# Giving the third x tile's transposes their own PSUM tiles and copies, at the start of a fused MLP forward and backward kernel

## The chip, the cores and the metric

The kernel runs on one NeuronCore of a Trainium2 chip. The metric is device time in microseconds (us), low is good. Each kernel was run several times; the median and the lowest and highest run are given. Where a ratio of two kernels is given, it is the mean time of one kernel's runs over the mean of the other's runs of the same rounds, with a 95% interval, so it is not quite the ratio of the medians quoted beside it. A profile is one execution recorded by the hardware profiler; its times count from the start of that execution's span.

## The reference

```python
B, S, D, F = 1, 2048, 640, 1536          # x, w1, w2, grad_out: bf16
def fwd(x, w1, w2):
    h = silu(einsum("bsd,df->bsf", x, w1))
    return einsum("bsf,fd->bsd", h, w2)
def reference(x, w1, w2, grad_out):
    out, vjp = jax.vjp(fwd, x, w1, w2)
    return (out, *vjp(grad_out))          # out, grad x, grad w1, grad w2
```

## The kernel before

The sequence is worked in four chunks of 512 rows. The first product, h = x w1, needs x transposed. For chunks 1 to 3 a DMA transposes it. For chunk 0 three x tiles of 128 rows are loaded plainly and transposed on TensorE (PE) against an identity; only the last 128 rows of the chunk come by DMA transpose (issued at 3.37 us in the trace of before, landing 4.9 us later, when the first matmul had long begun at 4.05). The first stage, `h_first`, then runs 40 matmuls of 384 columns, row block by row block of w1 (`dt_`), over eight output blocks (`ft`) at a time. The matmul that this document calls the ninth is the first one of the second w1 row block (`dt_ = 1`, `ft = 0`).

```python
P, NQ, SC, DT, NA, FC, FA = 128, 3, 512, 5, 8, 512, 1024
HC = NQ * P                                   # 384
# 18 warm-up matmuls on a tile of ones, from 0.51 to 2.61 us in the trace of before      ... cut
early += [load_x(nc.sync, 0), load_x(nc.scalar, 1), load_x(nc.sync, 2)]
early += [load_w1(0, slice(0, FC), nc.scalar), load_w1(0, slice(FC, FA))]
early += [load_w1(k, slice(0, FA)) for k in range(1, 3)]
for k in range(3, DT):
    load_w1(k, slice(0, FA))
nc.sync.dma_start_transpose(out=xT_next[:, :, HC:SC], in_=x2[HC:SC, :])
# ... cut: w2, grad_out and the transposed weights are loaded after these

def pe_x(xT):
    slices = ((0, 1), (1, 3), (3, DT))
    tps = [ps_h.tile([P, hi - lo, NQ, P], dt_in, name="tp", tag="hp") for lo, hi in slices]
    for q in range(NQ):
        for tp, (lo, hi) in zip(tps, slices):
            for dt_ in range(lo, hi):
                nc.tensor.transpose(tp[:, dt_ - lo, q, :], x_nat[:, q, dt_ * P:(dt_ + 1) * P], ident[:])
    for k, (tp, (lo, hi)) in enumerate(zip(tps, slices)):
        copy_tp = nc.scalar.copy if k % 2 else nc.vector.tensor_copy
        copy_tp(out=xT[:, lo:hi, 0:HC], in_=tp[:].rearrange("p k q s -> p k (q s)"))

def h_first(xT, aT, ghT):
    pe_x(xT)
    hs = [ps_h.tile([P, SC], FP32, name="hp") for _ in range(NA)]
    def mm(ft, dt_, cols, start, stop):
        nc.tensor.matmul(hs[ft][:, cols], lhsT=w1_nat[:, dt_, ft * P:(ft + 1) * P],
                         rhs=xT[:, dt_, cols], start=start, stop=stop)
    for dt_ in range(DT):
        for ft in range(NA):
            mm(ft, dt_, slice(0, HC), dt_ == 0, False)
    # ... cut: the last 128 columns, silu, the other four output blocks
```

## Time and profile before

| | before |
|---|---|
| time, first 3 runs | 320.03 us median (319.85 to 320.49) |
| span of the profiled execution | 317.7 us |
| PE busy | 313.2 us, 99% |

The first part of the page of the kernel before (busy us, share of the span and instructions of each engine) and its part on the chain of work that ended last:

```profile
PE 313.2 (99%) x1501; PEld 146.8 (46%) x1529; DVE 102.9 (32%) x182; ACT 77.2 (24%) x139; POOL 0.7 (0%) x6
...
PE 99%; issue 1%; DVE 0%; DVEq 0%
PE hp L299 32%; PE hp L283 16%; PE hp L388 16%; PE hp L439 15%; PE hp L220 13%; PE hp L251 3%; PE hp L419 1%; PE wp L162 1%; PE tp L211 0%; DVE xT L216 0%; DVE g L430 0%; DVE warm L158 0%; DVEq L430 0%; DVEq L467 0%
```

PE is busy for 99% of the span and the chain is PE from end to end. Time can be won only by giving PE less work, or by starting its useful work sooner. The change tries the second, so the first 6 us matter. The next fence is from the timeline of the kernel before (its first line is the heading: start in us, duration in us, engine, line, operation, output<-input, count, and in brackets the idle time before with what ended it). `tp` is the PSUM tile of the transposes, `w_nat` stands for w1 here (the profile leaves digits out of names), PEld is the weight load of the matmul that follows.

```profile
start us, us, engine line op out<-in xcount [idle before <-releaser]
...
2.43 1.39 PE L211 MATMUL tp<-ident,x_nat 128*128 128x128 bf16 x15
...
3.64 0.82 DVE L216 COPY xT<-tp 128x384 bf16<-128x384 bf16 x2 [3.19 <-PE tp L211]
3.73 0.10 PEld L251 LDWEIGHTS <-w_nat 128*128 128x128 bf16 x1
3.75 0.80 ACT L216 COPY xT<-tp 128x768 bf16<-128x768 bf16 x1 [1.06 <-PE tp L211]
4.05 9.15 PE L251 MATMUL hp<-xT,w_nat 128*128 128x384 bf16 x80 [0.23 <-DVE xT L216]
4.05 0.42 PEld L251 LDWEIGHTS <-w_nat 128*128 128x128 bf16 x3 [0.22 <-issue]
...
4.86 0.44 PEld L251 LDWEIGHTS <-w_nat 128*128 128x128 bf16 x4 [0.39 <-DMA w_nat<-in_w_dram]
...
5.59 7.44 PEld L251 LDWEIGHTS <-w_nat 128*128 128x128 bf16 x72 [0.29 <-DMA w_nat<-in_w_dram]
```

How to read it: the 15 transposes start at 2.43; the two DVE copies begin at 3.64 and the ACT copy at 3.75; the first 384-column matmul starts at 4.05, when the first DVE copy is done. After four weight loads (the one at 3.73 and three at 4.05) PE waits for a DMA until 4.86 (columns 512 to 1023 of the first w1 row block), and after four more it waits again until 5.59 (second row block). The 72 loads from there on show no wait. (In some fences below a count is cut at the end of the window that was asked for, as x43, or a record is missing from the trace, as in x79.)

Three numbers below this resolution come from the single records of the trace: the third x tile's DMA completed at 3.33; the first DVE copy (128x384) took 0.358 us and the second (128x768) 0.549; the two weight DMAs completed at 4.82 and 5.55.

### The profile page before, as it was taken

The page shows a single profiled execution, that of the slowest core. Times are in us where ns is not written, and L with a number is a line of the kernel's source. Part 1 is how long each engine was busy: PE and PEld are TensorE (multiplying, and loading weights), DVE is VectorE, ACT ScalarE, POOL GpSimd, SP SyncE. Part 2 cuts the span into 40 slices and gives each one's busy share as a digit, 9 for nine tenths or more (in the row PEclk, how much of TensorE's full clock was granted, in tenths as well). Part 3 has the DMA queues.
Part 4 walks back from the last instruction along what each step waited for, and adds up shares of the span by engine and source line. Part 5 has one row for each costly group of instructions (what it writes and reads, how often), then busy time and mean ns, then how long its engine had stood idle before and what let it go on. Part 6 is the DMA issues. An engine that isn't in the chain of part 4 may idle for free.

```text
span 317.7 us, 3605 instructions
## 1 busy us (share of the span) xinstructions
PE 313.2 (99%) x1501; PEld 146.8 (46%) x1529; DVE 102.9 (32%) x182; ACT 77.2 (24%) x139; POOL 0.7 (0%) x6
## 2 busy tenths in 40 slices
PE   9999999999999999999999999999999999999997
PEld 6644444444444444444444444444444444444444
DVE  1396631577310177700157741000000100001001
ACT  2592000654101354311064420111100001001110
POOL 0000000000000000000000000000000000000000
DMA  8989999999989885482644089919999999996011
GB/s 266 329 167 207 229 267 245 337 255 279 292 220 339 203 241 133 148 283 85 165 119 131 0 274 264 206 31 295 244 254 254 253 218 343 242 274 207 33 35 50
DMA packets 147264, 66.85 MB, mean 210 GB/s; under 512 B 113328, under 2 KB 146736, under 8 KB 147248
## 3 DMA queue, kind: packets, MB, share of 16 engines
q1 hardware_dynamic: 146960, 66.33, 82.0%
q10 hardware_dynamic: 288, 0.30, 0.3%
q8 instruction: 12, 0.20, 0.3%
q14 instruction: 4, 0.03, 0.0%
HBM read 9.18 MB, written 28.97 MB: 120 GB/s over the span
## 4 chain that ended last, share of the span: by engine, by line
PE 99%; issue 1%; DVE 0%; DVEq 0%
PE hp L299 32%; PE hp L283 16%; PE hp L388 16%; PE hp L439 15%; PE hp L220 13%; PE hp L251 3%; PE hp L419 1%; PE wp L162 1%; PE tp L211 0%; DVE xT L216 0%; DVE g L430 0%; DVE warm L158 0%; DVEq L430 0%; DVEq L467 0%
## 5 line engine op out<-in xcount | busy, mean ns | idle before, releaser
L283 PE MATMUL hp<-goT,w2T 128*128 128x512 bf16 x238 | 56.8, 380 | 0.1
L299 PE MATMUL hp<-aT,w_nat 128*128 128x512 bf16 x235 | 52.2, 379 | 0.3
L299 PE MATMUL hp<-ghT,w1T 128*128 128x512 bf16 x236 | 52.2, 379 | 0.2
L388 PE MATMUL hp<-a_blk,go_nat 128*128 128x512 bf16 x235 | 51.7, 379 | 0.3
L439 PE MATMUL hp<-gh_blk,x_nat 128*128 128x512 bf16 x220 | 48.3, 379 | 0.2
L220 PE MATMUL hp<-xT,w_nat 128*128 128x512 bf16 x192 | 47.8, 379 | 0.4
L307 ACT ACTIVATE oT<-hp 128x512 bf16<-128x512 f32 x24 | 14.4, 598 | 104.3 <-PE hp L299 104.3
L229 ACT ACTIVATE aT<-hp 128x512 bf16<-128x512 f32 x48 | 28.5, 614 | 37.2 <-PE hp L220 30.4
L283 PEld LDWEIGHTS <-w2T 128*128 128x128 bf16 x240 | 23.5, 98 | 28.3
L299 PEld LDWEIGHTS <-w_nat 128*128 128x128 bf16 x240 | 23.5, 98 | 28.3
L388 PEld LDWEIGHTS <-go_nat 128*128 128x128 bf16 x240 | 23.5, 98 | 28.3
L299 PEld LDWEIGHTS <-w1T 128*128 128x128 bf16 x240 | 23.4, 98 | 28.4
L290 DVE SCALAR_TENSOR_TENSOR ghT<-ghT,hp 128x512 bf16<-128x512 bf16 x48 | 32.5, 682 | 7.0 <-PE hp L283 7.0
L439 PEld LDWEIGHTS <-x_nat 128*128 128x128 bf16 x224 | 21.9, 98 | 26.5
L309 DVE CAST oT<-hp 128x512 bf16<-128x512 f32 x16 | 11.0, 690 | 70.6 <-PE hp L299 70.6
L236 DVE SCALAR_TENSOR_TENSOR ghT<-aT,v 128x512 bf16<-128x512 bf16 x48 | 32.6, 686 | 0.3
L220 PEld LDWEIGHTS <-w_nat 128*128 128x128 bf16 x200 | 19.5, 98 | 23.4
L235 DVE TENSOR_SCALAR v<-t 128x512 bf16<-128x512 f32 x48 | 20.1, 425 | 28.1 <-ACT t L233 28.1
L233 ACT ACTIVATE t<-hp 128x512 f32<-128x512 f32 x44 | 26.5, 620 | 0.0
L450 DVE CAST g<-hp 128x512 bf16<-128x512 f32 x7 | 4.8, 691 | 47.0 <-PE hp L439 28.2
L398 DVE CAST g2T<-hp 128x512 bf16<-128x512 f32 x7 | 4.8, 692 | 46.1 <-PE hp L388 46.1
L396 ACT ACTIVATE g2T<-hp 128x512 bf16<-128x512 f32 x8 | 4.8, 597 | 47.0 <-PE hp L388 47.0
(24 smaller groups left out, 42.0 us busy)
## 6 DMA issues: line engine op xcount, KB each, us to landing
aT_scr<-aT SPq DMA_DIRECT2D x4, 1536.0 KB, 6.2
ghT_scr<-ghT SPq DMA_DIRECT2D x4, 1536.0 KB, 8.0
out_dram<-o_sb SPq DMA_DIRECT2D x8, 640.0 KB, 3.7
oT_scr<-oT SPq DMA_DIRECT2D x4, 640.0 KB, 3.9
go_nat<-in_grad_out_dram SPq DMA_DIRECT2D x4, 640.0 KB, 7.7
gxT_scr<-oT SPq DMA_DIRECT2D x4, 640.0 KB, 5.2
w_nat<-in_w_dram SPq DMA_DIRECT2D x1, 1920.0 KB, 11.8
x_nat<-in_x_dram SPq DMA_DIRECT2D x3, 640.0 KB, 7.4
```

The source lines that it names most:

```text
L220: nc.tensor.matmul(hp[:], lhsT=w1_nat[:, dt_, ft * P:(ft + 1) * P], rhs=xT[:, dt_, :], start=(dt_ == 0), stop=(dt_ == DT - 1),)
L229: nc.scalar.activation(aT[:, ft, :], hp[:], ACT.Silu)
L233: nc.scalar.activation(t[:], hp[:], ACT.Tanh, scale=0.5)
L235: nc.vector.tensor_scalar(out=v[:], in0=t[:], scalar1=-0.5, scalar2=0.5, op0=ALU.mult, op1=ALU.add)
L236: nc.vector.scalar_tensor_tensor(out=ghT[:, ft, :], in0=aT[:, ft, :], scalar=1.0, in1=v[:], op0=ALU.subtract, op1=ALU.mult)
L283: nc.tensor.matmul(gp[:], lhsT=w2T[:, dt_, ft * P:(ft + 1) * P], rhs=goT[:, dt_, :], start=(dt_ == 0), stop=(dt_ == DT - 1),)
L290: nc.vector.scalar_tensor_tensor(out=ghT[:, ft, :], in0=ghT[:, ft, :], scalar=1.0, in1=gp[:], op0=ALU.add, op1=ALU.mult)
L299: nc.tensor.matmul(op_[:], lhsT=w_all[:, ft, dt_ * P:(dt_ + 1) * P], rhs=rhs_all[:, ft, :], start=(ft == 0), stop=(ft == FT - 1),)
L307: nc.scalar.activation(oT[:, dt_, :], op_[:], ACT.Copy)
L309: nc.vector.tensor_copy(out=oT[:, dt_, :], in_=op_[:])
L388: nc.tensor.matmul(gp[:], lhsT=go_nat[:, st, dt_ * P:(dt_ + 1) * P], rhs=a_blk[:, st, :], start=(st == 0), stop=(st == ST - 1),)
L439: nc.tensor.matmul(gp[:], lhsT=x_nat[:, st, dt_ * P:(dt_ + 1) * P], rhs=gh_blk[:, st, :], start=(st == 0), stop=(st == ST - 1),)
```

## The change

The third x tile arrives last. In the kernel before, one PSUM tile (the prediction says bank) holds all three tiles' transposes of the first row block, and one copy of 384 columns follows the last of them. The change copies the first two tiles' part ahead, while the third is still being transposed, so that after the last needed transpose a copy of only 128 columns stands before the first matmul. Four PSUM tiles are used for transposes in place of three.

```diff
-            slices = ((0, 1), (1, 3), (3, DT))
-            tps = [ps_h.tile([P, hi - lo, NQ, P], dt_in, name="tp", tag="hp") for lo, hi in slices]
-            for q in range(NQ):
+            slices = ((0, 1), (1, DT))
+            for qs in ((0, 1), (2,)):
+                tps = [ps_h.tile([P, hi - lo, len(qs), P], dt_in, name="tp", tag="hp") for lo, hi in slices]
+                for k, q in enumerate(qs):
+                    for tp, (lo, hi) in zip(tps, slices):
+                        for dt_ in range(lo, hi):
+                            nc.tensor.transpose(tp[:, dt_ - lo, k, :], ...)
                 for tp, (lo, hi) in zip(tps, slices):
-                    for dt_ in range(lo, hi):
-                        nc.tensor.transpose(tp[:, dt_ - lo, q, :], ...)
-            for k, (tp, (lo, hi)) in enumerate(zip(tps, slices)):
-                copy_tp = nc.scalar.copy if k % 2 else nc.vector.tensor_copy
-                copy_tp(out=xT[:, lo:hi, 0:HC], in_=...)
+                    copy_tp = nc.scalar.copy if lo and len(qs) > 1 else nc.vector.tensor_copy
+                    copy_tp(out=xT[:, lo:hi, qs[0] * P:(qs[-1] + 1) * P], in_=...)
```

(The elided arguments are as in the kernel before.) The instructions on PE keep their order.

More of the change, by code (lines that the diff above doesn't have):

```diff
@@ L205, in pe_x @@
         def pe_x(xT):
-            slices = ((0, 1), (1, 3), (3, DT))
-            tps = [ps_h.tile([P, hi - lo, NQ, P], dt_in, name="tp", tag="hp") for lo, hi in slices]
-            for q in range(NQ):
-                for tp, (lo, hi) in zip(tps, slices):
-                    for dt_ in range(lo, hi):
-                        nc.tensor.transpose(
-                            tp[:, dt_ - lo, q, :], x_nat[:, q, dt_ * P:(dt_ + 1) * P], ident[:]
-                        )
-            for k, (tp, (lo, hi)) in enumerate(zip(tps, slices)):
-                copy_tp = nc.scalar.copy if k % 2 else nc.vector.tensor_copy
-                copy_tp(out=xT[:, lo:hi, 0:HC], in_=tp[:].rearrange("p k q s -> p k (q s)"))
+            slices = ((0, 1), (1, DT))
[4 more added lines that the diff above has]
+                        for dt_ in range(lo, hi):
+                            nc.tensor.transpose(
+                                tp[:, dt_ - lo, k, :], x_nat[:, q, dt_ * P:(dt_ + 1) * P], ident[:]
+                            )
+                for tp, (lo, hi) in zip(tps, slices):
+                    copy_tp = nc.scalar.copy if lo and len(qs) > 1 else nc.vector.tensor_copy
+                    copy_tp(
+                        out=xT[:, lo:hi, qs[0] * P:(qs[-1] + 1) * P], in_=tp[:].rearrange("p k q s -> p k (q s)")
+                    )
         def h_mm(hp, ft, xT):
```

## The prediction

> **What bounds the kernel now.** The matmul engine: the profile's first table gives PE 313.2 of 317.7 us (99%), and the chain of waits is 99% PE. Only the start has anything to win. The timeline and its single records show (us from the span's start):
>
> - the third x tile lands at 3.33; its first transpose starts at 3.37; the transpose that the first copy needs ends at 3.60;
> - the first DVE copy, 128x384, runs 3.64 to 4.00 (0.358 us); the second, 128x768 in 0.549 us, ends at 4.46; the ACT copy, 128x768 in 0.798 us, ends at 4.55;
> - the first real matmul starts at 4.05, after that first copy; then one of 384 columns starts every 0.162 us;
> - the fifth needs columns 512 to 1023 of the first w1 row block. PE could take it at 4.70, but the DMA lands at 4.82 and the weight load starts at 4.86;
> - the ninth needs the second w1 row block. PE could take it at about 5.52; that DMA lands at 5.55, the load starts at 5.59.
> - After 5.59 no wait of PE in this stage is listed.
>
> **What the change does.** Transposes and matmuls stay the same, in the same order. The 384-column first copy becomes 256 + 128 columns on DVE; the two 128x768 copies become 128x1024 on ACT (first two x tiles) and 128x512 on DVE (third). Transposes use four PSUM banks, not three.
>
> Costs, estimated from the two DVE copies (about 0.17 us + 0.50 ns a column): 256 columns 0.29 us, done by 3.6, hidden under the third tile's transposes; 128 columns 0.23 us, 3.64 to 3.87; 512 columns 0.42 us, ending about 4.3. ACT, from 0.798 us for 768 columns and about 0.60 us for 512: 1.0 us for 1024, but starting 0.2 us sooner, so ending at about 4.55 as now. The first matmul then starts at about 3.92: 0.13 us sooner, not the 0.24 us of two thirds of the copy, because of DVE's fixed part.
>
> **How much is on the critical path.** Almost none. Four matmuls run 0.13 us earlier, then PE meets the same weights at 4.86 and 5.59; the wait before the fifth grows from 0.16 to about 0.29 us. The copies for the second row block are ready at 4.55, 1 us before its weights.
>
> On SP's queue one order changes, later: the first oT store goes ahead of the third chunk's xT load. Both come far ahead of use (that chunk starts near 108 us); I expect nothing.
>
> **Time.** 320.0 us before, 320.0 predicted; the gain is at most 0.13 us (0.04%), under the spread of the runs before (319.85 to 320.49). Range 319.6 to 320.4.
>
> **What would show it.** First 384-column matmul at about 3.9; the idle time before the fifth longer by as much; the ninth still at about 5.6, directly after its DMA; the span unchanged within 0.3 us.
>
> **What would make it wrong.** If in other executions the weights land over 0.2 us earlier against x, PE and not the DMA sets the ninth matmul, and the 0.13 us is saved. Also the clock: [...] Here transposes go from 0.106 to 0.055 us spacing at about 3.2; a later change would slow the first matmuls and take the DMA waits off the path. Either is worth tenths of a us.

## The result, and the profile after

| | before | after |
|---|---|---|
| median of 5 runs | 320.29 us (319.85 to 320.63) | 319.93 us (319.6 to 320.29) |
| ratio | | 0.9992, 95% interval 0.9978 to 1.0006 |
| span of the profiled execution | 317.7 us | 318.5 us |

The time is the same within the noise. Yet the profiled execution of the changed kernel was 0.8 us *longer* than that of the kernel before. The same parts of its page, and the same stretch of its timeline:

```profile
PE 315.5 (99%) x1529; PEld 147.5 (46%) x1529; DVE 103.0 (32%) x183; ACT 77.4 (24%) x139; POOL 0.7 (0%) x6
...
PE 98%; DMA 1%; DVE 0%; issue 0%; DVEq 0%; SPq 0%
PE hp L302 33%; PE hp L286 16%; PE hp L391 16%; PE hp L442 15%; PE hp L223 14%; PE hp L254 3%; PE hp L422 1%; DMA x_nat<-in_x_dram 1%; PE tp L212 1%; DVE g L433 0%; DVEq L433 0%; SPq L470 0%
```

(The first fence is the page, the second the timeline of the changed kernel.)

```profile
2.85 1.78 PE L212 MATMUL tp<-ident,x_nat 128*128 128x128 bf16 x15 [0.24 <-DMA x_nat<-in_x_dram]
...
3.72 0.29 DVE L217 COPY xT<-tp 128x256 bf16<-128x256 bf16 x1 [3.26 <-PE tp L212]
...
4.25 0.23 DVE L217 COPY xT<-tp 128x128 bf16<-128x128 bf16 x1 [0.24 <-PE tp L212]
...
4.53 9.50 PE L254 MATMUL hp<-xT,w_nat 128*128 128x384 bf16 x80
...
4.80 0.15 PEld L254 LDWEIGHTS <-w_nat 128*128 128x128 bf16 x1 [0.17 <-issue]
...
5.12 0.15 PEld L254 LDWEIGHTS <-w_nat 128*128 128x128 bf16 x1 [0.17 <-issue]
...
6.42 7.44 PEld L254 LDWEIGHTS <-w_nat 128*128 128x128 bf16 x72 [0.25 <-DMA w_nat<-in_w_dram]
```

(PE's busy time is not comparable between the two pages: the trace of before holds 1501 of the matmuls, that of after 1529.)

The change did what it was meant to do. DVE now copies 256 columns at 3.72, under the transposes, and the copy that the first matmul waits for takes 0.23 us (single record: 0.225, against 0.358). The first matmul starts 0.28 us after the start of that copy (4.25 to 4.53); before it was 0.41 us (3.64 to 4.05).

But nearly everything around it differs. The transposes start 0.42 us later because the first x tile landed later (at 2.81 in place of 2.39), and they take 1.78 us in place of 1.39. The weight loads from 4.80 on come 0.32 us apart, twice the 0.162 us of the kernel before. PE is at half clock: transposes start 0.107 us apart in place of 0.056, matmuls of 384 columns 0.320 in place of 0.162. ("Half clock" and "full clock" are names for these two spacings here. That the clock is behind them is a reading of the traces: the clock records of this trace begin at 5.71, with a granted share of 1.0, where the spacing falls to 0.162; there is none before, and the page counts that time as full clock. The trace of before has no clock record.) The single records show the change of speed: in this trace the half-clock spacing holds up to the matmul that starts at 5.12; in the trace of before, up to the transpose at 3.05. The fifth matmul's weights (DMA complete at 4.33) were not waited for at all. The ninth was: PE would have been free for it at about 6.39 (the eighth started at 6.23, plus 0.162), but its weights landed at 6.37 and its load started at 6.42. That is nearly a tie, 0.03 us: with the old copy, 0.133 us longer, PE would have come to the ninth matmul after its weights, so part of the saving (an estimate: at most 6.39 + 0.133 - 6.42 = 0.10 us) reached even this execution.

So two traces already show two things that set the ninth matmul's start and that the change does not touch: when PE leaves half clock, and when the weights land. The experiments ask which of them holds, how often, and whether the 0.13 us is there when neither does.

### The profile page after: what moved, and what is told of

Same layout as the page of the kernel before. It is cut to its first block, busy times and chain, and to the rows that moved or that the text cites. A ratio compares the mean times of both kernels' runs of the same rounds, so it can differ in the third digit from the quotient of the medians.

```text
span 318.5 us, 3634 instructions
## 1 busy us (share of the span) xinstructions
PE 315.5 (99%) x1529; PEld 147.5 (46%) x1529; DVE 103.0 (32%) x183; ACT 77.4 (24%) x139; POOL 0.7 (0%) x6
## 4 chain that ended last, share of the span: by engine, by line
PE 98%; DMA 1%; DVE 0%; issue 0%; DVEq 0%; SPq 0%
PE hp L302 33%; PE hp L286 16%; PE hp L391 16%; PE hp L442 15%; PE hp L223 14%; PE hp L254 3%; PE hp L422 1%; DMA x_nat<-in_x_dram 1%; PE tp L212 1%; DVE g L433 0%; DVEq L433 0%; SPq L470 0%
```

## The experiments

Three theories: A, the prediction's: the ninth matmul starts when the second w1 block lands, so a shorter copy only lengthens a wait. B: the first copy sets the start of the stage, and its saving reaches the end of every execution. C: the state at the start (clock, landings) is what moves the times from run to run.

The table collects all traces. "Half clock until" is the start of the last matmul or transpose that was followed at full half-clock spacing (0.105 us or more for 128 columns, 0.319 for 384); in the two traces marked "again" PE had been at full clock before and had fallen back (the last of the 110 warm-up matmuls ended by 9.00 and 8.83 us, under 0.08 us for each, less than the half-clock spacing of 0.107). All columns are us from the span's start, from the single records.

| trace | third x tile landed | half clock until | first matmul | second w1 block landed | ninth matmul | span |
|---|---|---|---|---|---|---|
| before | 3.33 | 3.05 | 4.05 | 5.55 | 5.60 | 317.7 |
| before_again | 3.51 | 5.74 | 4.51 | 4.90 | 6.67 | 318.7 |
| after | 3.63 | 5.12 | 4.53 | 6.37 | 6.42 | 318.5 |
| after_again | 3.58 | 4.04 | 4.35 | 5.38 | 5.67 | 317.7 |
| w_late | 3.47 | 3.81 | 4.25 | 7.92 | 7.96 | 320.1 |
| w_late_copy_late | 3.61 | 8.47 | 5.96 | 8.01 | 8.47 | 320.7 |
| copy_late | 3.50 | between 4.00 and 5.82 | 5.82 | 5.95 | 7.12 | 319.2 |
| before_w_ready | 3.45 | 3.79 | 4.23 | not used | 5.53 | 317.7 |
| after_w_ready | 3.89 | 4.81 | 4.54 | not used | 6.19 | 318.3 |
| few_warm | 3.55 | 5.96 | 4.41 | 5.27 | 6.65 | 318.7 |
| held_before | 3.54 | 14.74 (again) | 14.14 | 5.41 | 16.01 | 328.1 |
| held_after | 3.52 | 17.80 (again) | 14.00 | 5.17 | 16.52 | 329.5 |
| held2_before | 3.30 | 4.75 | 10.14 | 5.96 | 11.44 | 323.5 |
| held2_after | 3.48 | 5.92 | 10.01 | 5.35 | 11.30 | 323.4 |

One more fact from the records makes this table useful: from the start of the ninth matmul to the start of the last one of the kernel it is 309.59 us in the first traces of both kernels and 309.58 in their second traces. Everything that differs between these executions has happened by the ninth matmul; the other chunks, where one store and one load changed places on the queue of SP, add nothing.

### The two kernels once more: before_again and after_again

No edit. before_again:

> The kernel before once more, for a second trace. Theory A: ninth matmul within 0.05 us of the landing of the second w1 block if PE is at full clock by then. Rival C: clock change and x landing differ from the first trace (3.15 and 3.33 us) and move the span.

after_again:

> The changed kernel once more. Theory A: same as before within 0.15%; in the trace the ninth matmul starts within 0.05 us of the landing of the second w1 block unless PE still runs at half clock. Rival C (what moved the 5 runs is the state at the start: when PE leaves half clock and when the x tiles land): the trace shows another moment of the clock change than the first profile of this kernel (5.5 us) and the span moves with the ninth matmul's start, not with the copy.

Measured: after_again 320.10 us median (319.55 to 320.74, 6 runs) against 320.26 for the kernel before (11 runs), ratio 0.9996 (0.9967 to 1.0026). before_again 320.55 and 319.52 us in two runs. Timeline of the second trace of the kernel before:

```profile
4.10 0.98 DVE L216 COPY xT<-tp 128x384 bf16<-128x384 bf16 x2 [3.65 <-PE tp L211]
...
4.51 9.71 PE L251 MATMUL hp<-xT,w_nat 128*128 128x384 bf16 x79
...
5.42 0.15 PEld L251 LDWEIGHTS <-w_nat 128*128 128x128 bf16 x1 [0.17 <-issue]
5.74 0.15 PEld L251 LDWEIGHTS <-w_nat 128*128 128x128 bf16 x1 [0.17 <-issue]
...
6.06 8.03 PEld L251 LDWEIGHTS <-w_nat 128*128 128x128 bf16 x74 [0.17 <-issue]
```

And the changed kernel's second trace:

```profile
4.07 0.23 DVE L217 COPY xT<-tp 128x128 bf16<-128x128 bf16 x1 [0.24 <-PE tp L212]
4.15 8.94 PEld L254 LDWEIGHTS <-w_nat 128*128 128x128 bf16 x80
4.35 8.91 PE L254 MATMUL hp<-xT,w_nat 128*128 128x384 bf16 x80
```

In the kernel before, half clock lasted so long that no weight load waits for a DMA any more: the second w1 block had landed 1.8 us before the ninth matmul. In the changed kernel the clock rose about when the first matmul began, and all 80 weight loads follow each other without a wait; the second block landed at 5.38, 0.28 us before the ninth matmul started. In both of these PE itself, and with it the first copy, set the ninth matmul's start (the first matmul came 0.41 and 0.28 us after the start of that copy, as in the first traces). So theory A, and with it the step "then PE meets the same weights" of the prediction, holds in the first trace of each kernel and fails in the second trace of each. The expectation for before_again came with the condition that PE is at full clock, which was not so. That for after_again had the same condition, and there PE was at full clock: theory A's expectation of 0.05 us was plainly missed (0.28 us). And in the first trace of the changed kernel A held only by the 0.03 us worked out above.

### Weights late, copy late: w_late, copy_late, w_late_copy_late

w_late puts a third of the w2 load ahead of the second w1 block in the kernel before:

```diff
         early += [load_w1(0, slice(0, FC), nc.scalar), load_w1(0, slice(FC, FA))]
+        early += [nc.sync.dma_start(out=w2_nat[:, 0:4, :], in_=w2_v[:, 0:4, :])]
         early += [load_w1(k, slice(0, FA)) for k in range(1, 3)]
-        nc.sync.dma_start(out=w2_nat[:], in_=w2_v[:])
+        nc.sync.dma_start(out=w2_nat[:, 4:FT, :], in_=w2_v[:, 4:FT, :])
```

> The kernel before, with a third of the w2 load (640 KB) moved ahead of the second w1 row block. At the 0.69 us per 256 KB at which the w1 blocks landed one after another in the trace of before (5.55, 6.21, 6.85), the second block should land about 1.7 us later, near 7.3. Theory A (the ninth matmul of the first stage starts when the second w1 block lands): ninth matmul directly after that landing, span about 1.7 us longer than before (ratio about 1.005). Rival B (the first copy sets the start of the stage, the weights only follow): span longer by clearly less, since the copy is untouched.

Measured: 321.92 us median (321.51 to 324.05, 6 runs) against 320.26, ratio 1.0056 (1.0023 to 1.0088). The timeline of w_late:

```profile
4.25 1.46 PE L252 MATMUL hp<-xT,w_nat 128*128 128x384 bf16 x8
...
7.96 6.10 PEld L252 LDWEIGHTS <-w_nat 128*128 128x128 bf16 x48 [2.64 <-DMA w_nat<-in_w_dram]
7.96 6.21 PE L252 MATMUL hp<-xT,w_nat 128*128 128x384 bf16 x47 [2.25 <-DMA w_nat<-in_w_dram]
```

The second block landed at 7.92 (expected near 7.3, 0.6 us sooner; the three landings that the expectation quotes are 0.65 us apart, not 0.69, and in the four traces of the two plain kernels the block landed anywhere from 4.90 to 6.37) and the ninth matmul started 0.05 us later, after PE had stood for 2.25 us. Compared with the first trace of before, ninth matmul and span moved by the same 2.4 us. Here the weights were last, and they set the time, to the full amount.

copy_late puts three copies into a scratch tile ahead of the first x copy of the kernel before:

```diff
+            idle = cpool.tile([P, HC], dt_in, name="idle")
+            for _ in range(3):
+                nc.vector.tensor_copy(out=idle[:], in_=tps[0][:].rearrange("p k q s -> p (k q s)"))
             for k, (tp, (lo, hi)) in enumerate(zip(tps, slices)):
```

> The kernel before with the same three scratch copies ahead of the first x copy, weights as they were. Delay of the first matmul about 1.4 us. Theory A: the first 0.2 us of it vanish in the wait for the weights, the rest is paid: span about 1.2 us longer than before (ratio about 1.0038). Rival B: all of it, 1.4 us. The two differ by less than the noise of the times, so the trace decides: ninth matmul not waiting for a DMA, and 8 x 0.162 us after the first (at full clock).

Measured: 321.70 us median (320.81 to 322.94, 6 runs), ratio 1.0041 (1.0008 to 1.0074). The timeline of copy_late, from the copy that the first matmul needs:

```profile
5.42 0.35 DVE L219 COPY xT<-tp 128x384 bf16<-128x384 bf16 x1
...
5.82 8.27 PEld L254 LDWEIGHTS <-w_nat 128*128 128x128 bf16 x71 [1.57 <-issue]
```

The first matmul came at 5.82, later than estimated, and all weight loads of this stage ran through; the ninth matmul started 1.30 us after the first, which is 8 x 0.162. Against the first trace of before, the first matmul is 1.77 us later and the ninth 1.52 us: 0.25 us vanished in waits for weights, as A expected. But that comparison is with one trace, and before_again shows that another would give another number. What is firm is that here the copy, which was last (5.42 to 5.77), set the first matmul and with it the ninth.

w_late_copy_late joins both edits:

> As w_late, and three copies into a scratch tile stand ahead of the first x copy on DVE, so that it ends about 1.4 us later (estimate from 0.36 and 0.55 us copies with their overlap) and the first matmul starts near 5.5. Theory A: the ninth matmul still starts at the landing of the second w1 block (about 7.3), so no longer than w_late: difference under 0.2 us. Rival B: about 1.4 us longer than w_late.

Measured: 322.58 us median (321.85 to 324.32, 6 runs), 0.66 us over the median of w_late (0.51 us in the means), between the 0 of A and the 1.4 of B. The runs of the two overlap over most of their range (321.51 to 324.05 and 321.85 to 324.32), so the times alone exclude neither. Its timeline:

```profile
5.96 8.23 PE L255 MATMUL hp<-xT,w_nat 128*128 128x384 bf16 x43 [1.40 <-DVE xT L220]
...
8.15 0.15 PEld L255 LDWEIGHTS <-w_nat 128*128 128x128 bf16 x1 [0.17 <-DMA w_nat<-in_w_dram]
8.47 0.15 PEld L255 LDWEIGHTS <-w_nat 128*128 128x128 bf16 x1 [0.17 <-issue]
```

The trace tells why the run is inconclusive for A: after 1.40 us without a matmul, PE was at half clock through all eight matmuls (weight loads 0.32 us apart), so PE reached the ninth at 8.47, after its weights (8.01). At full clock it would have been ready at 7.26 (5.96 plus 8 x 0.162, an estimate) and would have waited for them. The delay of the copy was about two thirds absorbed here, by 1.71 us later at the first matmul and 0.51 at the ninth.

### Weights never waited for: before_w_ready, after_w_ready

Wrong result on purpose: the 384-column matmuls take all their weights from the piece that the first one needs.

```diff
-                    lhsT=w1_nat[:, dt_, ft * P:(ft + 1) * P],
+                    lhsT=w1_nat[:, 0, ft % FB * P:(ft % FB + 1) * P] if cols.start == 0
+                    else w1_nat[:, dt_, ft * P:(ft + 1) * P],
```

> Wrong result on purpose: the first stage's 384-column matmuls all use the first 512 columns of the first w1 row block as weights, so that none but the first waits for a weight DMA. Kernel before otherwise. Theory A: in the trace eight matmuls run without a break, the ninth 1.30 us after the first (at full clock), about 0.24 us less than before; span shorter by about 0.2 us at most. Rival B: no difference in the span.

> The same with the changed kernel. Theory A: only here does the shorter copy show: the ninth matmul, counted from the landing of the third x tile, comes about 0.13 us sooner than in before_w_ready when both traces run at the same clock. The times can't resolve that (spread 0.7 us). Rival B: the same 0.13 us, but it should then also be there with the true weights.

Measured: before_w_ready 319.66 us median (319.5 to 320.46, 6 runs), ratio 1.0000 (0.9985 to 1.0014). after_w_ready 319.92 us (319.25 to 320.45, 6 runs), ratio 0.9997 (0.9981 to 1.0012). Both are wrong by design (relative error 0.48). In the trace of before_w_ready the ninth matmul comes 1.30 us after the first, as expected. In that of after_w_ready half clock lasted into the first matmuls, so that the distance was 1.66 us, and the pair can't be compared for the 0.13 us; the times can't show it either. What follows is modest: taking away every wait for weights behind the first gained nothing that 6 runs can show, so those waits cost less than about 0.15% in the mean. But that bound is 0.48 us, more than the 0.25 us of waits in the first trace of before, so this run decides nothing between the theories. From the start of the needed copy to the first matmul it was 0.41 us in one and 0.28 us in the other, as in all other traces of either kind (0.40 to 0.41 and 0.28).

### The clock: few_warm

The changed kernel with `NWARM = 2` in place of 18.

> The changed kernel with 2 warm-up matmuls in place of 18, so that PE is nearly idle until the x tiles land. Rival C (the clock): half clock lasts longer after the first transposes (until about 5.5 us or later in all executions), the first eight matmuls take up to 0.32 us each, the ninth starts at 6.3 or later, not waiting for a DMA; times longer by 0.3 to 0.8 us than the changed kernel. If the clock did not matter: within 0.1 us of the changed kernel.

Measured: 320.74 us median (320.39 to 322.75, 6 runs) against 319.74 for the kernel before in the same rounds (11 runs), ratio 1.0035 (1.0014 to 1.0057). The timeline of few_warm:

```profile
4.41 9.79 PE L254 MATMUL hp<-xT,w_nat 128*128 128x384 bf16 x79
...
5.97 0.15 PEld L254 LDWEIGHTS <-w_nat 128*128 128x128 bf16 x1 [0.17 <-issue]
...
6.29 7.79 PEld L254 LDWEIGHTS <-w_nat 128*128 128x128 bf16 x73 [0.17 <-issue]
```

Half clock lasted until 5.96, no weight load waited for a DMA, and the ninth matmul came at 6.65 although its weights were there at 5.27. The late clock change comes with about 1 us here (320.74 against 319.74), some seven times what the shorter copy can save. (The comparison is with the kernel before, which shared the rounds; the changed kernel itself was in the rounds of another chip.)

### Both kernels held back until clock and weights are ready: held and held2

To see the copy alone, the transposes were made to wait for an identity that is ready only after a row of small DVE copies, while more warm-up matmuls keep PE busy. The same edit was made to both kernels:

```diff
-    NWARM = 18
+    NWARM = 110            # held2: 90
         make_identity(nc, ident[:])
+        for _ in range(48):    # held2: 33
+            nc.vector.tensor_copy(out=turn[:], in_=warm[:])
+        nc.vector.scalar_tensor_tensor(out=ident_late[:], in0=ident[:], scalar=1.0, in1=turn[:],
+                                       op0=ALU.mult, op1=ALU.mult)
         # ... the transposes use ident_late
```

> The kernel before with its start held back: 48 small DVE copies stand before the identity that all transposes need, and 110 warm-up matmuls keep PE busy meanwhile, so that x, the w1 blocks and the clock are all ready when the transposes begin (near 8 us, estimate). Rival C says that the moment of the clock change and the landings make the spread of the times: it should fall from about 1 us to about 0.3 us or less. In the trace: transposes at 0.055 us, first matmul 0.41 us after the start of the first copy, and eight matmuls without a break.

> The changed kernel held back in the same way. All agree on the trace: first matmul 0.28 us after the start of its copy. With weights and clock out of the way theory A (the saving is lost only where a weight block lands late) says that the whole 0.13 us reaches the ninth matmul and the span: median 0.13 us under held_before, if the spread allows it to be seen. If the saving were also lost elsewhere (a later copy of 1024 or 512 columns, a PSUM bank freed late), the ninth matmul would come at the same distance from the start of the transposes in both.

Measured: held_before 330.98 us median (329.9 to 331.43, 4 runs), held_after 330.06 us (329.94 to 331.31, 5 runs). The spread did not fall. The identity came later than estimated, at 12.3 us, as the timeline of held_before and then that of held_after show:

```profile
12.36 1.76 PE L218 MATMUL tp<-ident_late,x_nat 128*128 128x128 bf16 x15 [3.37 <-DVE ident_late L170]
...
14.14 6.10 PE L258 MATMUL hp<-xT,w_nat 128*128 128x384 bf16 x33
...
14.74 0.15 PEld L258 LDWEIGHTS <-w_nat 128*128 128x128 bf16 x1 [0.17 <-issue]
15.06 0.15 PEld L258 LDWEIGHTS <-w_nat 128*128 128x128 bf16 x1 [0.17 <-issue]
```

```profile
12.36 1.76 PE L219 MATMUL tp<-ident_late,x_nat 128*128 128x128 bf16 x15 [3.52 <-DVE ident_late L170]
...
14.00 6.22 PE L261 MATMUL hp<-xT,w_nat 128*128 128x384 bf16 x24
```

PE had been without a matmul for 3.4 us and was back at half clock: transposes in 1.76 us, matmuls 0.32 us apart. That was after 3.37 us (held_before) and 3.52 us (held_after) without a matmul; after 2.25 us (w_late) PE was not at half clock (eight matmuls from 7.96 on, 0.16 us apart). Where between the two it falls back, these runs do not show. So the test of the spread failed by its own making. Yet the first matmul, with the transposes starting at 12.36 in both, came at 14.14 and at 14.00. That lead did not reach the ninth matmul: it came at 16.01 in held_before and at 16.52 in held_after, because half clock ended 3 us later there. So the lower median of held_after (0.92 us) is no measure of the copy. The second pair shortens the hold:

> As held_before, with 33 DVE copies (0.232 us each there) and 90 warm-up matmuls, so that the transposes begin near 8.7 us, under 2.5 us after the last warm-up matmul, and PE does not fall back to half clock as it did after 3.4 us without work in held_before. Rival C: spread of the times 0.3 us or less. In the trace: transposes every 0.055 us, first matmul 0.41 us after the start of its copy, ninth 1.30 us after the first, no DMA wait.

> The changed kernel held in the same way. If the 0.13 us of the shorter copy reach the end wherever neither weights nor clock interfere: first and ninth matmul 0.13 us sooner after the start of the transposes than in held2_before, and median time 0.13 us lower (visible if the spread falls to 0.3 us). If it is lost at another place (the 1024-column ACT copy, the 512-column DVE copy, a bank freed late): ninth matmul at the same distance in both and equal times.

| | held2_before | held2_after |
|---|---|---|
| runs (us) | 325.30, 325.32, 325.32, and one of 326.99 | 325.15, 325.15, 325.16, 325.16, 325.16 |
| median | 325.32 | 325.16 |
| transposes start | 8.920 | 8.918 |
| first matmul | 10.141 | 10.006 |
| ninth matmul | 11.438 | 11.303 |
| last matmul | 321.022 | 320.887 |

The timelines of held2_before and of held2_after:

```profile
8.92 1.00 PE L218 MATMUL tp<-ident_late,x_nat 128*128 128x128 bf16 x15 [1.15 <-DVE ident_late L170]
...
9.73 0.82 DVE L223 COPY xT<-tp 128x384 bf16<-128x384 bf16 x2 [0.86 <-PE tp L218]
...
10.14 8.89 PE L258 MATMUL hp<-xT,w_nat 128*128 128x384 bf16 x80 [0.22 <-DVE xT L223]
```

```profile
8.92 1.00 PE L219 MATMUL tp<-ident_late,x_nat 128*128 128x128 bf16 x15 [0.59 <-DVE ident_late L170]
...
9.45 0.93 DVE L224 COPY xT<-tp 128x256 bf16<-128x256 bf16 x3 [0.58 <-PE tp L219]
9.67 1.01 ACT L224 COPY xT<-tp 128x1024 bf16<-128x1024 bf16 x1 [6.99 <-PE tp L219]
...
10.01 8.89 PE L261 MATMUL hp<-xT,w_nat 128*128 128x384 bf16 x80
```

This settles what the copy is worth. With clock and weights ready, the spread of the changed kernel's runs falls from 0.7 and 1.2 us (its two plain sets) to 0.01 us, and three of the four runs of the other lie within 0.02 us. (The fourth, 326.99, had a mean granted clock of 0.995 in place of 1.0. The runs of held_before and held_after, whose traces show PE back at half clock, have 0.99 and 0.995 too, so a relapse is likely; no trace of this run exists, and its cause is not shown.) The two kernels then differ by 0.135 us at the first matmul, at the ninth and at the last (0.002 of it is the start of the transposes; the rest, 0.133, is what the needed copy is shorter), and by 0.16 us in the medians. The pair holds clock and landings still together, so it does not say how much of the spread is due to each. The copies of 1024 columns on ACT (9.67, 1.01 us) and of 512 on DVE take nothing back. The hold itself costs 5 us (325.32 against 319.94 for the kernel before in the same rounds), so neither version is of use as a kernel, and no run pointed to one that beats both originals.

## Why the prediction was right or wrong

**The time: right.** 320.0 was predicted and 319.93 measured, inside the range. That is no support for the mechanism: had the whole 0.13 us been saved every time, about 319.9 would have been predicted, inside the same range. The number would have come out right under theory A or B.

**The size of the saving: right.** The prediction worked out 0.13 us for the shorter copy, from the two DVE copies before. Measured: 0.135 us in the held2 pair. The single costs were right too: 256 columns 0.292 us (predicted 0.29), 128 columns 0.225 (0.23), 512 columns 0.424 (0.42), 1024 columns on ACT 1.012 (1.0). The copies on DVE of 128 to 512 columns lie on one line, 0.52 ns a column on top of 0.158 us (worked out from 0.225 us for 128 columns and 0.358 for 384; it gives 0.292 for 256 and 0.424 for 512, as measured, and 0.557 for 768, measured 0.549). The prediction had 0.50 ns and 0.17 us from two copies. The difference, 0.133 us, is the slope alone: 256 columns less.

**Where the saving goes: right only for a part of the executions.** The step that failed is "Four matmuls run 0.13 us earlier, then PE meets the same weights at 4.86 and 5.59". It read one trace as if it were every execution. In before and after, the ninth matmul was held by its weights (it started 0.05 us after their landing), in after by 0.03 us only. In before_again and after_again, it was not; PE set it, and there the copy is on the critical path. The signs that the prediction named for the profile fared accordingly: the first profile of the changed kernel had the first matmul at 4.53 (predicted 3.9), no wait before the fifth (a longer one was predicted), the ninth at 6.42 directly after its DMA (5.6 predicted; the releaser as predicted, but PE itself would have been free 0.03 us earlier), and a span 0.8 us longer (within 0.3 predicted).

**What would make it wrong: both things happened, and larger.** The prediction said that another moment of the clock change or other landings are worth tenths of a us. They are worth more: the ninth matmul moved between 5.60 and 6.67 in four traces of the two kernels. The median stayed in the range all the same: both kernels show a scatter of this kind, and the gain of 0.13 us at most is 0.04% of the time. The scatter of the clock change was the term that was mis-sized: the last half-clock spacing began at 3.05, 5.74, 5.12 and 4.04 us in the four traces, up to 2.7 us apart, with the same 18 warm-up matmuls.

**What stays open.** How often each limit holds can't be told from four traces. If the moment of the clock change does not move with an earlier start, which no run shows, such a start is worth about half where PE is at half clock (an estimate from the spacings of 0.32 and 0.162 us). In the plain kernels the gain of one execution is then between 0 and 0.135 us (argued; no run measures it), which fits both measured ratios (0.9992 and 0.9996) but is proved by neither.

## What to carry to other kernels

Before trusting a slack of a few tenths of a us that one trace shows, look at a second trace of the same kernel: which wait ends last at a kernel's start can change from execution to execution (here the ninth matmul of one kernel waited for its weights in one trace, and in the other they had landed 1.8 us before it). When a change is smaller than the spread of the runs, find what makes the spread and hold it still in both versions (here clock and loads, by starting later); then 0.13 us in 325 could be measured with four and five runs. And count a shortened copy at its slope alone: a third of the columns took 63% of the time, as 0.225 against 0.358 us.
